# Transfers of 48, 48 and 2 partitions joined into one of 98, and halves of 64 into one of 128, in a Fourier and expert kernel

## The chip, the cores and the metric

The kernel runs on one core of one Trainium2 chip. The metric is the device time of one execution, in microseconds. "Before" is the median of 3 runs. The rows shown come from one profiled execution of the same program.

## What is computed

The input `x` has 8 batches of 3136 rows and 256 columns, in f32. Each batch goes through a real FFT along its rows, a complex 256x256 product with a bias and a soft threshold, and the inverse FFT. Then the 128 rows with the highest gate score go through a small network and are written back in place.

```python
X = np.fft.rfft(x, axis=1)
Yr = Xr @ w_r - Xi @ w_i + b_r
Yi = Xr @ w_i + Xi @ w_r + b_i
Y  = soft threshold of Yr and Yi by 0.01
y  = np.fft.irfft(Y, n=3136, axis=1)
scores = y @ w_gate
top = the 128 rows of the batch with the highest score
y[top] += sigmoid(scores[top]) * (relu(y[top] @ w1) @ w2)
```

## The kernel before

The row index is split as 3136 = 98 x 32, and each transform is done in two stages of matrix products with a transposition between them. The transposition goes through DRAM: the scratch tensor `As[b]` lies between the two forward stages, `Cs[b]` between the two inverse ones. Each tensor of a batch (`x`, `As` written, `As` read, `Cs` written, `Cs` read, output) has 3136 rows of 1 KB, so a batch moves six times 3.1 MB.

- `ld_x` loads a block of `x` (a quarter of a batch) into a tile of 8 KB a partition. 98 classes of rows lie in two groups of 49, at partitions 0 to 48 and 64 to 112. The helper `rows` makes three transfers of it: 48 partitions from 64 on, 48 partitions from 0 on, and the two left over (48 and 112).
- `fold` (GpSimd; VectorE for part of batch 0) makes sums and differences of a block, `s1` multiplies them by the first-stage table `w1f` (TensorE, then a copy to the tile `at` on ScalarE or VectorE), and every second `s1` writes `at` to `As[b]`, through `rows` again (three transfers).
- `ld_a` reads `As[b]` for two steps at a time into the tile `av` (two buffers), in two transfers of 64 partitions. `s2` multiplies it by `g_sb` into the PSUM tile `pm`; ScalarE, VectorE and GpSimd split the result into the high and low parts `Xh` and `Xl`.
- `spectral` is the 256x256 complex product in three passes each (`mm3`, lines 233 to 235), the bias and the threshold. `s2i` is the first inverse stage; it writes `Cs[b]` from `ct` in four transfers of 64 partitions and 128 KB each, for every second step.
- `ld_c` reads `Cs[b]` into the tile `cv` (through `rows`, three transfers), `s1i` is the last stage, and every second `s1i` writes a block of the output from `ot` (through `rows`).

A batch has 13 steps (`G`), and the loop at the end of the function writes out an order by hand: at iteration t come `s1` of a later batch, `ld_a` for step t+2, `ld_x`, `ld_c`, `s2` of step t+1, `s2i` of step t-2, `s1i` of step t-17, and `spectral` of step t, with pieces of routing (`route`: scores, a search for the threshold, the places of the chosen rows) and of the network (`ffn`) between them. Nearly all transfers are issued on SyncE's queue (SP), which works in order. Those issued by `ld` are chained one behind the other; those issued by `put` are placed by the scheduler. Each transfer on SP waits for a semaphore, and eight semaphores go round: a transfer waits until the one issued eight before it has landed.

`place` works out the row numbers of the chosen rows with a chain of small VectorE operations, that ends at line 327.

Of the kernel before, what the change touches and what calls it, by code (L numbers as in the profile page):

```python
# [23 lines left out]
H1 = 49  # L24
LAM = 0.01


def _slots(j):
    out = []
    for a in range(2):  # L30
        if j == NJ - 1:
            out += [(a, False, 49 * a + 98 * k2, 1.0, k2) for k2 in range(17 - a)]
        else:
            for k2 in range(N2):
                k = 2 * j + 2 - a + 98 * k2
                out.append((a, True, k, 1.0 if 2 * k <= S else -1.0, k2))
    return out


def _tables():  # L40
    n1 = np.arange(N1)
    n2 = np.arange(N2)
    w1 = np.zeros((2, H1, N1))
    for a in range(2):
        for j in range(NJ - 1):
            t = 2 * np.pi * ((n1 * (2 * j + 2 - a)) % N1) / N1
            w1[a, 2 * j] = np.cos(t)
            w1[a, 2 * j + 1] = -np.sin(t)
        w1[a, H1 - 1] = 1.0 - 2.0 * a * (n1 % 2)
    g = np.zeros((NJ, 2, 2, N2, 2, N2))  # L50
    gi = np.zeros((NJ, 2, 2, N2, 2, N2))
    for j in range(NJ):
        for a, cplx, k, sg, s in _slots(j):
            t = 2 * np.pi * ((n2 * k) % S) / S
            co, si = np.cos(t), np.sin(t)
            if cplx:
                g[j, a, 0, :, 0, s] = co
                g[j, a, 1, :, 0, s] = si
                g[j, a, 0, :, 1, s] = -sg * si
                g[j, a, 1, :, 1, s] = sg * co  # L60
                gi[j, a, 0, s, 0] = 2 * co / S
                gi[j, a, 1, s, 0] = -2 * sg * si / S
                gi[j, a, 0, s, 1] = 2 * si / S
                gi[j, a, 1, s, 1] = 2 * sg * co / S
            else:
                edge = k in (0, S // 2)
                g[j, a, 0, :, 0, s] = co
                gi[j, a, 0, s, 0] = (1.0 if edge else 2.0) * co / S
                if not edge:
                    g[j, a, 0, :, 1, s] = -si  # L70
                    gi[j, a, 1, s, 0] = -2 * si / S
    main = [v[:NJ - 1].reshape(NJ - 1, 128, 64).transpose(1, 0, 2) for v in (g, gi)]
    g_last = np.zeros((2, N2, 2, 64))
    gi_last = np.zeros((2, 2, N2, 2, N2))
    for a in range(2):
        g_last[a, :, a] = g[NJ - 1, a, 0].reshape(N2, 64)
        gi_last[a, :, :, a] = gi[NJ - 1, a, :, :, 0]
    wf = np.zeros((128, 2, 64))
    wi = np.zeros((128, 64))
    for r in (0, 64):  # L80
        wf[r:r + H1, :, :H1] = w1[:, :, :H1].transpose(2, 0, 1)
    for a in range(2):
        wi[64 * a:64 * a + H1, :H1] = w1[a, :, :H1]
    wq = np.zeros((NJ, 2, 2, N1))
    for gg in range(6):
        for e in range(2):
            for f in range(2):
                for a in range(2):
                    j = 4 * gg + 2 * e + f
                    wq[4 * gg + 2 * f + a, e] = w1[a, 2 * j:2 * j + 2]  # L90
    wq[NJ - 1, 0] = w1[:, H1 - 1]
    return (wf, wi, main[0], main[1], g_last.reshape(64, 2, 64), gi_last.reshape(128, 64), wq.reshape(NJ, 4, N1))
# [19 lines left out]
def fourier_moe(ctx: ExitStack, tc: tile.TileContext, x, w_r, w_i, b_r, b_i, wg, w1, w2,  # L112
# [25 lines left out]
    w1f, w1i = c_tile([128, 2, 64], F32, "w1f"), c_tile([128, 64], F32, "w1i")  # L138
# [69 lines left out]
    def consts_moe(k):  # L208
# [7 lines left out]
        else:  # L216
# [3 lines left out]
            nc.gpsimd.iota(nrow, [[1, 1]], base=0, channel_multiplier=N2, allow_small_or_imprecise_dtypes=True)  # L220
# [61 lines left out]
    def place(b, thr, slots):  # L282
# [25 lines left out]
        for k in range(NCHK):  # L308
# [18 lines left out]
            nc.vector.tensor_tensor(out=idx, in0=c, in1=pi[:, N2 + 1:], op=ALU.add)  # L327
# [86 lines left out]
    def s1(b, i):  # L414
        if i == 0:
            As[b] = dram.tile([2, H1, N2, D], F32, name="As")
# [14 lines left out]
        if i % 2 == 1:  # L431
            rows(put if b else ld, at[b], As[b][:, :, 4 * i - 4:4 * i + 4, :], True)

    def jrows(t, a, j0, n):
        return t[a, 2 * j0:2 * j0 + 2 * n].rearrange("(j q) n d -> (q n) j d", q=2)

    def ld_a(b, g):
        if g == G - 1:
            av[b, g] = pool.tile([64, 1, D], F32, name="av", bufs=2)
            for a in range(2):  # L440
                ld(av[b, g][N2 * a:N2 * a + N2, 0, :], As[b][a, H1 - 1])
        elif g % 2 == 0:
            av[b, g] = av[b, g + 1] = pool.tile([128, 4, D], F32, name="av", bufs=2)
            for k in range(0, 4, 2 if b + g == 0 else 4):
                n = 2 if b + g == 0 else 4
                for a in range(2):
                    ld(av[b, g][64 * a:64 * a + 64, k:k + n, :], jrows(As[b], a, 2 * g + k, n))

    def s2(b, g):
        v = av.pop((b, g))  # L450
        w = width(g)
        px = pm[:, :, :256]
        for p in range(w):
            for h in range(2):
                for e in range(2):
                    for a in range(2):
                        o = px[64 * e:64 * e + 64, a, 64 * (2 * p + h):64 * (2 * p + h) + 64]
                        c = slice(128 * h + 64 * e, 128 * h + 64 * e + 64)
                        if w == 2:
                            r = slice(64 * a, 64 * a + 64)  # L460
                            main_pe[0] = nc.tensor.matmul(o, v[r, 2 * (g % 2) + p, c], g_sb[r, 2 * g + p, :], start=True, stop=True).ins  # L461
                        else:
                            main_pe[0] = nc.tensor.matmul(o, v[:, 0, c], g_last[:, a, :], start=True, stop=True).ins
# [275 lines left out]
```

## Time and profile before

| what | value |
|---|---|
| runs | 995.34, 999.82, 990.12 us (median 995.34) |
| the profiled execution | 992.02 us, of which the span of the trace is 989.7 us |
| mean granted TensorE clock | 0.866 of full speed |
| TensorE busy | 747.6 us (76% of the span) |
| VectorE, ScalarE, GpSimd busy | 535.1, 321.0, 247.0 us |
| moved by the DMA engines | 162.40 MB, 164 GB/s over the span |

The span runs from the first to the last instruction of the core; the 2.3 us outside it are start and end of the execution. Busy TensorE time counts a matmul at either clock. "DMA share" is the mean busy share of the 16 DMA engines; since packets overlap it can read a little over 1.

### The profile page before, as it was taken

What the parts mean: (1) busy time and instruction counts of PE and PEld (TensorE: products, weight loads), DVE (VectorE), ACT (ScalarE), POOL (GpSimd) and SP (SyncE); (2) the same over time, 40 slices, a digit from 0 to 9 for tenths busy, and PEclk for the clock granted to TensorE, in tenths of its full rate; (3) what the DMA queues carried; (4) which work ended last, traced back from release to release, by engine and by line L of the source; (5) the groups of instructions that cost most, each with busy time, mean ns of one, the idle gap of its engine ahead of it and who ended that gap; (6) DMA issues with size and microseconds to landing.
All of it is one profiled execution on the core that took longest, in us unless ns stands there. A gap on an engine that the chain in (4) does not pass through costs nothing.

```text
span 989.7 us, 20397 instructions
## 1 busy us (share of the span) xinstructions
PE 747.6 (76%) x8090; PEld 553.4 (56%) x8090; DVE 535.1 (54%) x1434; ACT 321.0 (32%) x622; POOL 247.0 (25%) x359
## 2 busy tenths in 40 slices
PE   4797888776867787679757986787767867776786
PEld 1375676554745465556546664656546656564456
DVE  5334544445444445345847784654555766766642
ACT  1133333333433433235323442432333332322111
POOL 3054442213133323233322332302300101110001
PEclk9778988888888889789978997979789998988778
DMA  9779788878888787778777877777284773536621
GB/s 172 184 148 216 195 180 162 205 182 219 191 193 189 182 190 210 160 208 194 193 165 189 213 177 172 180 186 160 67 203 102 162 147 79 117 83 137 154 52 46
DMA packets 84188, 162.40 MB, mean 164 GB/s; under 512 B 10593, under 2 KB 64510, under 8 KB 77822
## 3 DMA queue, kind: packets, MB, share of 16 engines
q1 hardware_dynamic: 83054, 158.88, 69.5%
q0 software_dynamic: 896, 2.17, 0.7%
q8 instruction: 64, 1.05, 0.5%
q14 instruction: 30, 0.25, 0.1%
q10 hardware_dynamic: 144, 0.07, 0.0%
HBM read 83.02 MB, written 78.12 MB: 163 GB/s over the span
## 4 chain that ended last, share of the span: by engine, by line
PE 35%; DMA 25%; DVE 15%; SPq 11%; ACT 6%; issue 5%; POOL 1%; POOLq 0%; DVEq 0%; ACTq 0%
DMA av<-As 9%; DMA cv<-Cs 8%; DMA xt<-in_x 7%; SPq L395 6%; PE py L233 5%; PE py L235 5%; SPq L170 5%; PE py L234 4%; PE s L560 4%; PE pm L461 4%; PE s L425 3%; PE s L514 3%; DVE py L489 3%; DVE junk L521 2%; DVE ot L565 1%
## 5 line engine op out<-in xcount | busy, mean ns | idle before, releaser
L461 PE MATMUL pm<-g_sb,av 64*64 64x64 f32 x3072 | 86.7, 244 | 135.0 <-DMA av<-As 103.8
L474 POOL TENSOR_SCALAR Xl<-Xl 128x256 fp32r<-128x256 f32 (+1 forms) x104 | 41.4, 398 | 574.2 <-DVE Xl L473 556.1
L473 DVE TENSOR_TENSOR Xl<-pm,Xh 128x512 fp32r<-128x512 f32 (+1 forms) x104 | 69.6, 669 | 205.4 <-ACT Xh L472 193.4
L461 PEld LDWEIGHTS pm<-g_sb,av 64*64 64x64 f32 x3072 | 73.0, 153 | 186.3 <-issue 78.0
L491 ACT ACTIVATE r<-py,m2l 128x512 f32<-128x512 f32 (+1 forms) x104 | 69.8, 671 | 329.0 <-DVE py L489 215.7
L410 POOL TENSOR_TENSOR x<-xt 113x512 f32<-113x512 f32 x116 | 145.9, 1290 | 25.7 <-DMA xt<-in_x 23.4
L233 PE MATMUL py<-wrh,Xh 128*128 128x256 f32 x400 | 133.2, 333 | 0.0
L233 PEld LDWEIGHTS py<-wrh,Xh 128*128 128x128 f32 x400 | 83.6, 209 | 69.3 <-issue 63.1
L235 PE MATMUL py<-wrl,Xh 128*128 128x256 f32 x400 | 121.3, 303 | 0.0
L234 PE MATMUL py<-wrh,Xl 128*128 128x256 f32 x400 | 120.0, 300 | 0.0
L233 PE MATMUL py<-wih,Xh 128*128 128x256 f32 x400 | 116.6, 291 | 0.0
L234 PE MATMUL py<-wih,Xl 128*128 128x256 f32 x400 | 116.0, 290 | 0.0
L235 PE MATMUL py<-wil,Xh 128*128 128x256 f32 x400 | 115.3, 288 | 0.0
L470 ACT CAST Xh<-pm 128x512 fp32r<-128x512 f32 (+1 forms) x104 | 59.7, 574 | 162.4 <-PE pm L461 147.4
L489 DVE TENSOR_TENSOR py<-py,bias 128x512 f32<-128x512 f32 (+1 forms) x104 | 70.4, 677 | 61.3 <-PE py L235 46.7
L425 PE MATMUL s<-x,w1f 49*64 49x512 f32 x512 | 86.1, 678 | 19.5 <-DVE x L410 13.4
L521 DVE CUSTOM_DVE_ANT_0 junk<-s,wgb 128x256 f32<-128x256 f32 (+1 forms) x200 | 84.4, 422 | 23.9 <-ACT ct L516 19.2
L493 DVE SCALAR_TENSOR_TENSOR Y<-py,r 128x512 f32<-128x512 f32 (+1 forms) x104 | 69.6, 669 | 49.5 <-ACT r L491 49.2
L560 PE MATMUL s<-cv,w1i 49*64 49x512 f32 x480 | 86.2, 731 | 6.7 <-DMA cv<-Cs 5.1
L235 PEld LDWEIGHTS py<-wrl,Xh 128*128 128x128 f32 x400 | 83.8, 210 | 7.5 <-issue 7.2
L234 PEld LDWEIGHTS py<-wrh,Xl 128*128 128x128 f32 x400 | 84.5, 211 | 0.0
L565 DVE TENSOR_TENSOR ot<-even,s 113x512 f32<-113x512 f32 x120 | 78.5, 680 | 7.6 <-ACT even L563 7.5
(117 smaller groups left out, 1186.8 us busy)
## 6 DMA issues: line engine op xcount, KB each, us to landing
xt<-in_x SPq DMA_DIRECT2D x64, 384.0 KB
Cs<-ct SPq DMA_DIRECT2D x192, 128.0 KB
av<-As SPq DMA_DIRECT2D x94, 256.0 KB
As<-at SPq DMA_DIRECT2D x60, 384.0 KB
cv<-Cs SPq DMA_DIRECT2D x60, 384.0 KB
out<-ot SPq DMA_DIRECT2D x60, 384.0 KB
As<-ot SPq DMA_DIRECT2D x4, 384.0 KB
xt<-Cs SPq DMA_DIRECT2D x4, 384.0 KB
```

Of the source, the lines that this page charges most:

```text
L233: nc.tensor.matmul(out, wh, mh, start=start, stop=False)
L234: nc.tensor.matmul(out, wl, mh, start=False, stop=False)
L235: return nc.tensor.matmul(out, wh, ml, start=False, stop=stop).ins
L410: ins = eng.tensor_tensor(out=xs[b, i][:H2, k], in0=t[:, 0], in1=t[:, 1], op=op).ins
L425: main_pe[0] = nc.tensor.matmul(p[64 * e:64 * e + 64, u, :], w1f[r, e, :], x2[r, e, :], start=True, stop=True).ins
L461: main_pe[0] = nc.tensor.matmul(o, v[r, 2 * (g % 2) + p, c], g_sb[r, 2 * g + p, :], start=True, stop=True).ins
L473: step_ins["x"] = nc.vector.tensor_tensor(out=part(xl, 0, 0, 64), in0=pv, in1=part(xh, 0, 0, 64).bitcast(F32), op=ALU.subtract).ins
L489: nc.vector.tensor_tensor(out=py, in0=py, in1=bias.rearrange("p (o d) -> p o d", o=1).broadcast_to([128, w, D]), op=ALU.add)
L491: nc.scalar.activation(out=r1, in_=py, func=AF.Relu, bias=m2l, scale=1.0)
L521: nc.vector.tensor_tensor_reduce(out=junk[:r], in0=p[:r, a, D * f:D * f + D], in1=wgb[:r], scale=1.0, scalar=0.0, op0=ALU.mult, op1=ALU.ad ...
L560: main_pe[0] = nc.tensor.matmul(p[64 * u:64 * u + 64, a, :], w1i[r], c[r, u, o:o + 2, :].rearrange("p c d -> p (c d)"), start=True, stop=T ...
L565: nc.vector.tensor_tensor(out=ot[b][:H2, t, o:o + 2, :].rearrange("p c d -> p (c d)"), in0=even[:H2], in1=p[:H2, 1, :], op=op)
```

## The change

The 98 classes of rows are paired anew, so that a class has its row in one list of 98 for both scratch tensors (`As[b]` and `Cs[b]` become [98, 32, 256]), and they sit on the neighbouring partitions 15 to 112 (`R0` to `H2`) of each tile. With that:

- `x` is laid out on the host by blocks: a block is 98 neighbouring rows of 8 KB in DRAM, and `ld_x` is one transfer of 98 partitions. The output is laid out in the same way, and put back in order on the host.
- A write of `As`, a read of `Cs` and a write of the output are one transfer of 98 partitions each, in place of three. In DRAM a row of such a transfer is 8 KB for all of them; in `As` and `Cs` the rows lie 32 KB apart, as before.
- A read of `As` is one transfer of 128 partitions and 512 KB, in place of two of 64 partitions; a write of `Cs` is one of 128 partitions, in place of four of 64. Their pieces stay at 1 KB.
- The products of `s1` and `s1i` contract over partitions 0 to 63 and 64 to 112; partitions 0 to 14 meet zero weights, and the six tiles of `ring` and `ring_c` are cleared there once at the start (before: three tiles). The number and sizes of all other matmuls stay.
- `cv` becomes three fixed tiles (`ring_c`), one of which takes the fourth block of batch 0, so that all four blocks of batch 0 are loaded at once.
- `Xh` and `Xl` are laid out so that the first copy and the difference are one contiguous piece.
- `place` needs three more small VectorE operations for the new row numbers.

```diff
-    def blocks(v):
-        return v.rearrange("(t n k u c) d -> k u n t (c d)", t=2, n=H1, u=2, c=4)
-
-    def rows(f, t, d, store):
-        for a, b in [(t[64 * u:64 * u + H1 - 1], d[u, :H1 - 1]) for u in (1, 0)] + [(t[H1 - 1:H2:64], d[:, H1 - 1])]:
-            f(b, a) if store else f(a, b)
...
     def ld_x(b, i):
         if i % 2 == 0:
             k = i // 2
-            xt[b, i] = xt[b, i + 1] = ring[(4 * b + k) % XB]
-            if b == 0 and k < XB:
-                (nc.vector, nc.gpsimd)[k % 2].memset(xt[b, i][32:64], 0.0)
-            rows(ld, xt[b, i].rearrange("p t c d -> p t (c d)"), blocks(x[b])[k], False)
+            xt[b, i] = xt[b, i + 1] = ring[(4 * b + k) % XB] if 4 * b + k != XB else ring_c[0].rearrange("p (t c) d -> p t c d", t=2)
+            ld(xt[b, i][R0:H2], x[b, k])
...
+        p_in = (slice(0, 64), slice(64, H2))
...
-                r = slice(64 * u, 64 * u + H1)
+                r = p_in[u]
                 main_pe[0] = nc.tensor.matmul(p[64 * e:64 * e + 64, u, :], w1f[r, e, :], x2[r, e, :], start=True, stop=True).ins
...
-            rows(put if b else ld, at[b], As[b][:, :, 4 * i - 4:4 * i + 4, :], True)
-
-    def jrows(t, a, j0, n):
-        return t[a, 2 * j0:2 * j0 + 2 * n].rearrange("(j q) n d -> (q n) j d", q=2)
+            (put if b else ld)(As[b][:, 4 * i - 4:4 * i + 4, :], at[b][R0:H2])
+
+    def steps(t, g, n):
+        r = H1 * (g // 6) + 8 * (g % 6)
+        return t[r:r + 4 * n].rearrange("(j q) n d -> (q n) j d", q=4)
...
-            for k in range(0, 4, 2 if b + g == 0 else 4):
+            for k in range(0, 2, 1 if b + g == 0 else 2):
                 n = 2 if b + g == 0 else 4
-                for a in range(2):
-                    ld(av[b, g][64 * a:64 * a + 64, k:k + n, :], jrows(As[b], a, 2 * g + k, n))
+                ld(av[b, g][:, 2 * k:2 * k + n, :], steps(As[b], g + k, n))
...
-            for e in range(2):
-                for a in range(2):
-                    nc.sync.dma_start(out=jrows(Cs[b], a, 2 * (g - 1 + e), 2), in_=ct[64 * e:64 * e + 64, :, a, :])
+            put(steps(Cs[b], g - 1, 4), ct.rearrange("p f a d -> p (f a) d"))
...
-            rows(put, cv[b, 2 * k], Cs[b][:, :, 8 * k:8 * k + 8, :], False)
+            cv[b, 2 * k] = cv[b, 2 * k + 1] = ring[k - 2].rearrange("p t c d -> p (t c) d") if b == B - 1 and k > 1 else ring_c[(4 * b + k) % XB]
+            put(cv[b, 2 * k][R0:H2], Cs[b][:, 8 * k:8 * k + 8, :])
...
-            rows(put, ot[b].rearrange("p t c d -> p t (c d)"), blocks(outs[b])[i // 2], True)
+            put(outs[b].rearrange("(k p t c) d -> k p t c d", k=4, t=2, c=4)[i // 2], ot[b][R0:H2])
...
+    ring_c = [pool.tile([128, 8, D], F32, name=f"cv{k}", bufs=1) for k in range(XB)]
+    for k, t in enumerate(ring + ring_c):
+        (nc.vector, nc.gpsimd)[k % 2].memset(t[:32], 0.0)
...
-    for i in range(2 * XB):
+    for i in range(U):
         ld_x(0, i)
...
-            nc.vector.tensor_tensor(out=idx, in0=c, in1=pi[:, N2 + 1:], op=ALU.add)
+            f4 = pool.tile([n, 1], U32, name="f4")
+            nc.vector.tensor_copy(f4, c)
+            nc.vector.tensor_scalar(out=f4, in0=f4, scalar1=2, scalar2=None, op0=ALU.logical_shift_right)
+            nc.vector.tensor_tensor(out=c, in0=c, in1=pi[:, N2 + 1:], op=ALU.add)
+            nc.vector.scalar_tensor_tensor(out=idx, in0=f4, scalar=float(8 * H1 - 4), in1=c, op0=ALU.mult, op1=ALU.add)
```

## Rows read from the trace of the kernel before

**Rows 1.** The page: span, and busy time of each engine.

```profile
span 989.7 us, 20397 instructions
...
PE 747.6 (76%) x8090; PEld 553.4 (56%) x8090; DVE 535.1 (54%) x1434; ACT 321.0 (32%) x622; POOL 247.0 (25%) x359
```

**Rows 2.** The page: chain of work that ended last, by line.

```profile
DMA av<-As 9%; DMA cv<-Cs 8%; DMA xt<-in_x 7%; SPq L395 6%; PE py L233 5%; PE py L235 5%; SPq L170 5%; PE py L234 4%; PE s L560 4%; PE pm L461 4%; PE s L425 3%; PE s L514 3%; DVE py L489 3%; DVE junk L521 2%; DVE ot L565 1%
```

**Rows 3.** Busy time by stretch: length, engines (instructions), clock, DMA share, GB/s.

```profile
0.00:45.00 45.00, 28.65 (x120) 10.51 (x120) 20.35 (x34) 5.39 (x6) 8.29 (x14) 0.89 0.82 174
45.00:130.00 85.00, 70.35 (x818) 57.00 (x818) 37.99 (x81) 30.75 (x60) 39.16 (x50) 0.84 0.84 190
...
331.00:436.00 105.00, 78.59 (x935) 58.99 (x935) 50.58 (x114) 37.25 (x72) 30.92 (x46) 0.85 0.80 190
...
645.00:778.00 133.00, 102.87 (x1064) 76.60 (x1068) 67.68 (x202) 42.30 (x83) 23.68 (x38) 0.87 0.61 142
...
891.00:990.00 99.00, 72.20 (x427) 49.81 (x422) 48.03 (x149) 15.72 (x31) 6.91 (x7) 0.80 0.42 97
```

**Rows 4.** TensorE's waits, whole run: us in total, times, longest.

```profile
PE pm L461 <- DMA av<-As: 103.8, 43, 7.5
```

**Rows 5.** The same for 130 to 436 us, then for 436 to 645 us.

```profile
PE pm L461 <- DMA av<-As: 61.8, 24, 7.5
...
PE pm L461 <- DMA av<-As: 27.6, 10, 6.8
```

**Rows 6.** Timeline of SP, then of TensorE, around one such wait.

```profile
410.13 2.24 SPq L395 DMA_DIRECT2D As<-at  x3
412.42 1.16 SPq L170 DMA_DIRECT2D av<-As  x1
...
418.19 1.02 PE L461 MATMUL pm<-g_sb,av 64*64 64x64 f32 x27 [5.83 <-DMA av<-As]
```

**Rows 7.** Busy time before, in and after that wait, columns as in rows 3.

```profile
405.50:411.50 6.00, 6.00 (x80) 4.50 (x79) 4.00 (x7) 2.31 (x5) 3.78 (x5) 1.00 0.46 109
412.00:418.00 6.00, 0.35 (x3) 0.19 (x2) 1.39 (x2) 0.69 (x1) 0.00 (x0) 0.70 0.90 214
418.00:424.00 6.00, 5.81 (x70) 5.02 (x70) 2.42 (x9) 2.15 (x4) 0.75 (x2) 0.73 0.97 277
```

**Rows 8.** Stretches in which one kind of transfer runs: x, cv, As, Cs, av, w1s, out.

```profile
5.00:18.00 13.00, 7.33 (x28) 2.16 (x30) 6.87 (x16) 1.01 (x1) 2.94 (x2) 1.00 1.05 176
262.40:265.60 3.20, 3.20 (x66) 2.33 (x59) 1.09 (x2) 2.70 (x6) 0.00 (x0) 1.00 1.09 182
249.20:251.20 2.00, 2.00 (x9) 1.54 (x8) 1.02 (x3) 0.93 (x4) 0.48 (x3) 0.50 1.06 213
404.00:406.20 2.20, 2.20 (x19) 2.20 (x19) 1.58 (x6) 0.00 (x0) 2.20 (x3) 0.96 0.95 203
406.80:407.40 0.60, 0.60 (x8) 0.22 (x9) 0.60 (x1) 0.00 (x0) 0.60 (x2) 1.00 0.93 302
192.40:193.40 1.00, 1.00 (x10) 0.49 (x5) 0.71 (x3) 0.59 (x2) 0.74 (x2) 0.92 1.04 406
267.60:269.20 1.60, 0.54 (x35) 0.43 (x30) 1.29 (x5) 0.18 (x1) 0.00 (x0) 1.00 1.01 397
```

**Rows 9.** Issues on SP by tile: ns of one, min/median/max; first and last start.

```profile
L170 SPq DMA_DIRECT2D av<-As x114: 307/616/1886, 40.6 to 869.3; - x114
L395 SPq DMA_DIRECT2D As<-at x84: 302/422/2377, 67.3 to 743.5; - x84
...
L529 SPq DMA_DIRECT2D Cs<-ct x192: 574/607/1508, 74.1 to 902.4; - x192
```

**Rows 10.** Timeline of the start: VectorE's clearing of a tile; TensorE's last pair of `s1`.

```profile
1.32 1.76 DVE L402 MEMSET xt<- 32x2048 f32 x1 [0.46 <-issue]
...
28.13 4.17 PE L425 MATMUL s<-x,w1f 49*64 49x512 f32 x16 [2.01 <-DVE x L410]
```

**Rows 11.** Groups by line: VectorE's last operation of `place`.

```profile
L327 DVE TENSOR_TENSOR idxs<-col,pm 128x1 uint32<-128x1 f32 x8 | 1.2, 154 | 0.2
```

More of the change, by code (lines that the diff above doesn't have):

```diff
@@ L24, with _slots @@
 H1 = 49
+R0 = 15
+H2 = 113
 LAM = 0.01
-def _slots(j):
-    out = []
-    for a in range(2):
[L31 to L37, printed above, removed]
+def _slots(i, a):
+    if i == 24:
+        return [(False, 49 * a + 98 * k2, 1.0, k2) for k2 in range(17 - a)]
+    ks = [2 * i + 2 - a + 98 * k2 for k2 in range(N2)]
+    return [(True, k, 1.0 if 2 * k <= S else -1.0, s) for s, k in enumerate(ks)]
 def _tables():
@@ L44, in _tables @@
     for a in range(2):
[L45 to L48, printed above, removed]
+        for i in range(24):
+            t = 2 * np.pi * ((n1 * (2 * i + 2 - a)) % N1) / N1
+            w1[a, 2 * i] = np.cos(t)
+            w1[a, 2 * i + 1] = -np.sin(t)
         w1[a, H1 - 1] = 1.0 - 2.0 * a * (n1 % 2)
-    g = np.zeros((NJ, 2, 2, N2, 2, N2))
-    gi = np.zeros((NJ, 2, 2, N2, 2, N2))
@@ L52, in _tables @@
[L52 to L71, printed above, removed]
@@ L72, in _tables @@
-    main = [v[:NJ - 1].reshape(NJ - 1, 128, 64).transpose(1, 0, 2) for v in (g, gi)]
+    g = np.zeros((2, 25, 2, N2, 2, N2))
+    gi = np.zeros((2, 25, 2, N2, 2, N2))
+    for a in range(2):
+        for i in range(25):
+            for cplx, k, sg, s in _slots(i, a):
+                t = 2 * np.pi * ((n2 * k) % S) / S
+                co, si = np.cos(t), np.sin(t)
+                if cplx:
+                    g[a, i, 0, :, 0, s] = co
+                    g[a, i, 1, :, 0, s] = si
+                    g[a, i, 0, :, 1, s] = -sg * si
+                    g[a, i, 1, :, 1, s] = sg * co
+                    gi[a, i, 0, s, 0] = 2 * co / S
+                    gi[a, i, 1, s, 0] = -2 * sg * si / S
+                    gi[a, i, 0, s, 1] = 2 * si / S
+                    gi[a, i, 1, s, 1] = 2 * sg * co / S
+                else:
+                    edge = k in (0, S // 2)
+                    g[a, i, 0, :, 0, s] = co
+                    gi[a, i, 0, s, 0] = (1.0 if edge else 2.0) * co / S
+                    if not edge:
+                        g[a, i, 0, :, 1, s] = -si
+                        gi[a, i, 1, s, 0] = -2 * si / S
@@ new lines, in _tables @@
+    tg = np.zeros((2, 64, 24, 64))
+    tgi = np.zeros((2, 64, 24, 64))
+    wq = np.zeros((NJ, 2, 2, N1))
+    for st in range(12):
+        a, c = st // 6, 4 * (st % 6)
+        for j in range(2):
+            for p in range(2):
+                tg[p, :, 2 * st + j] = g[a, c + 2 * j + p].reshape(64, 64)
+                tgi[j, :, 2 * st + p] = gi[a, c + 2 * j + p].reshape(64, 64)
+                r = 2 * (c + 2 * j + p)
+                wq[2 * st + j, p] = w1[a, r:r + 2]
+    wq[NJ - 1, 0] = w1[:, H1 - 1]
@@ L451, in s2 @@
         w = width(g)
-        px = pm[:, :, :256]
-        for p in range(w):
+        for j in range(2):
             for h in range(2):
                 for e in range(2):
[L456 to L463, printed above, removed]
@@ L464, in s2 @@
-        xh, xl = pair([128, 2 * w, 2, 128], "X", 2)
-        pv = px[:, :, :128 * w].rearrange("p a (t c) -> p a t c", c=64)
+                    c = slice(128 * h + 64 * e, 128 * h + 64 * e + 64)
+                    for p in range(w):
+                        o = pm[64 * e:64 * e + 64, p, 128 * h + 64 * j:128 * h + 64 * j + 64]
+                        r = slice(64 * p, 64 * p + 64)
+                        lhs, rhs = (v[r, 2 * (g % 2) + j, c], g_sb[r, 2 * g + j, :]) if w == 2 else (v[:, 0, c], g_last[:, j, :])
+                        main_pe[0] = nc.tensor.matmul(o, lhs, rhs, start=True, stop=True).ins
@@ L467, in part @@
+        xh, xl = pair([128, 2, 2 * w, 128], "X", 2)
+        pv = pm[:, :w, :256].rearrange("p a (t c) -> p a t c", c=64)
         def part(t, k, lo, hi):
-            return t[:, :, k, :].rearrange("p t (a c) -> p a t c", a=2)[:, :, :, lo:hi]
-        nc.scalar.copy(out=part(xh, 0, 0, 64), in_=pv)
+            return t[:, k].rearrange("p (a h) (j c) -> p a (h j) c", a=w, j=2)[:, :, :, lo:hi]
+        whole = [t[:, 0].rearrange("p (a h) c -> p a (h c)", a=w) for t in (xh, xl)]
+        nc.scalar.copy(out=whole[0], in_=pm[:, :w, :256])
@@ L524, in s2i @@
             for a in range(2):
-                nc.sync.dma_start(out=Cs[b][a, H1 - 1], in_=ct[N2 * a:N2 * a + N2, 0, 0, :])
+                put(Cs[b][H1 * a + H1 - 1], ct[N2 * a:N2 * a + N2, 0, 0, :])
         else:
-            for e in range(2):
-                for a in range(2):
-                    nc.sync.dma_start(out=jrows(Cs[b], a, 2 * (g - 1 + e), 2), in_=ct[64 * e:64 * e + 64, :, a, :])
+            put(steps(Cs[b], g - 1, 4), ct.rearrange("p f a d -> p (f a) d"))
     def score(b):
@@ L737 @@
     r = _run(nc, [arrays], core_ids=[0])
-    return np.stack([r.results[0][f"out_{b}"] for b in range(B)])
+    o = np.stack([r.results[0][f"out_{b}"] for b in range(B)])
+    return np.ascontiguousarray(o.reshape(B, 4, 2, H1, 2, 4, D).transpose(0, 4, 3, 1, 2, 5, 6).reshape(B, S, D))
```

66 lines of the change are left out of this document (30 added, 36 removed).

## The prediction, made before the changed kernel was run

> **What bounds the kernel now.** I read the page first. TensorE is the busiest engine, with 747.6 of 989.7 us [rows 1]; no engine is full, so something makes it wait. The chain that ended last names it: transfers and SP's queue (av 9%, cv 8%, xt 7%, the issues of lines 395 and 170 another 11%) take more of it than any line of TensorE [rows 2]. Then busy time by stretch. In one batch of the steady part, 331 to 436 us, TensorE works 78.6 of 105 us while the 16 DMA engines are busy for 0.80 of it, and the granted clock is 0.85 [rows 3]. Of TensorE's waits one stands out: `s2` waits for `av`, 103.8 us in 43 waits, with 7.5 us the longest [rows 4]; 61.8 us of it fall in 24 waits between 130 and 436 us [rows 5]. In 436 to 645 us it is 27.6 us, because the search for the threshold brings other waits.
>
> One such wait shows the mechanism [rows 6]. SP issues the three pieces of an `As` write from 410.13 on, and this takes until 412.37; only then the second half of `av` is issued, at 412.42. TensorE starts on it at 418.19, after 5.83 us of idleness. So the wait is made of SP's issuing, of the `As` bytes ahead in the DMA engines, and of `av` itself. [...]
>
> **The DMA engines.** I looked for stretches in which one kind of transfer runs with the engines full (share near 1) [rows 8]. Loads into 48 partitions are slow: x 176 GB/s, cv 182. The write of `As` from 48 partitions has 213 in its first 2 us. `Cs` has 203, which is about SP's pace, since one of its 131 KB pieces is issued every 607 ns [rows 9] (216 GB/s). `av` has 302. One load into 128 partitions, w1s, has 406, and the write of the output 397. A block is 803 KB (98 rows of 8 KB; 786 KB for `av` and `Cs`), so it now costs x 4.6, cv 4.4, As 3.8, out 2.0, av 2.6, Cs 3.9, together 21.3 us. This agrees with 0.80 of 105 us for four blocks, 21.0 us [rows 3].
>
> After the change x is a load into neighbouring partitions from neighbouring rows, like w1s: I take 354 GB/s, the middle of 302 and 406, so 2.3 us (bounds 2.0, and the 5.2 of the slow rival below). The output takes the same 2.3 us, 0.3 more than now. For cv the destination becomes wide as for w1s while the 8 KB rows stay 32 KB apart in DRAM; no row parts the two, so I take 3.2 us, at 250 GB/s between 354 and 182 (bounds 2.0 and 5.0). For `As` the output shows that rows 32 KB apart can be written at 397, its own row says 213; I take 3.0 us (bounds 2.0 and 4.3). `av` keeps its 1 KB pieces and 2.6 us (bound 1.9 at 406). `Cs` has pieces of the same size and loses SP's pace: 2.6 us (bounds 1.9 and 3.9). Sum 16.0 us a block, bounds 11.8 and 23.3.
>
> [...]
>
> **The wait for av.** Per block SP issues 1 `As` for 3, 1 x, 1 cv and 1 output for 3 each; per two steps 1 `Cs` for 4 and 1 `av` for 2. In the wait above, one `As` issue of 0.42 us [rows 9] for the 2.24 brings `av` forward by 1.8 us. The `As` bytes ahead take 3.0 for 3.8 us, 0.8 less. If `av` stays behind `As` and its first half can no longer go ahead (it is one transfer), its extra 262 KB at 302 GB/s cost 0.9 us. Net 1.7 us less, up to 2.6 where both halves were behind anyway; with a mean wait of 61.8/24 = 2.6 us I take two thirds of the waits as gone: 69 of 103.8 us (bounds: a quarter if `As` takes 4.3 us, and all).
>
> **The clock.** [...]
>
> **Start.** Today's first piece of x goes to partitions from 64 on and waits for nothing; the new first load covers cleared partitions and waits for VectorE's first clearing, until 3.1 us [rows 10]. But four blocks at 176 GB/s take 18 us, at 354 they take 9. The last pair of `s1` starts at 28.13 after waits; four pairs of 4.2 us back to back from about 9 us would start the last at 21.6. I take 6 us (bounds 2 and 9). Three more clearings lie beside the first loads' flight and cost nothing; if VectorE were late for the first `fold`, 1.8 us each.
>
> **End, and edits with small answers.** The last batch reads four blocks of `Cs` at once before its `s1i`: 4 us less if they follow the sum, of which I take 2. `place` has three more operations of 0.154 us [rows 11], only exposed in the last batch: 0.5 us more; in the others VectorE has room (50.6 of 105 us). Matmuls keep number and size; the contraction over 64 for 49 partitions changes no column count, so I cost it at nothing (bounds plus or minus 2 us). The copies to `Xh` and `Xl` have as many elements: nothing, plus or minus 3 us in all, hidden behind `spectral` of the step before.
>
> **What is late next.** When `av` is on time, TensorE meets the chains of ScalarE and VectorE, and the other waits of the search. In 331 to 436 us TensorE is idle for 26.4 us, and about 21 of them are `av` (61.8 x 105/306); 5 us a batch belong to others already. I add 3 us a batch for six batches, 18 us (bounds 5 and 40). The DMA engines would be busy for 64 us of a batch of some 89, so 0.72, no longer the limit.
>
> **Sum.** -69 - 38 - 6 - 2 + 0.5 + 18 = -96.5 us, from the profiled 992.0 to 895.5. The median is 3.3 us above that execution, so 899 us.
>
> **Rivals.** (1) The DRAM side, not the partitions, makes cv and `As` slow. For: x, cv and `As` all have rows 32 KB apart in DRAM, `av` and w1s have not. Against: the output has them, and 397 GB/s. Then only x gains; a block is 2.3 + 5.0 + 4.3 + 2.3 + 2.6 + 2.6 = 19.1 us, SP's issues still shrink, `av` comes 1.8 - 0.5 us earlier and 45% of the waits go: -47 - 20 + 5 = about -62, 933 us. (2) Slower: fewer engines a transfer. The 48-partition transfers keep all 16 engines busy (share 1.05 for x [rows 8]), 3 partitions each. 98 doesn't divide by 16; if 98 partitions are dealt out as 14 shares of 7, two engines stand idle. If moreover each engine keeps today's pace, x, cv and `As` have 154, 159 and 186 GB/s, a block costs 23.3 us, and a batch at today's share of 0.80 takes 93/0.80 = 116 us for 105: 11 us on each of 5.7 batches, 63 us, 1058 us. It decides as soon as a block costs more than 21.3 us, that is if x, cv and `As` stay under some 190 GB/s on average. Against: w1s runs at 406 on the same engines. (3) The waits vanish wholly and the DMA engines have 11.8 us a block: -104 - 51 - 9 - 4 + 15 = -153, 842 us. (4) The scheduler moves the single `av` issue behind `As` and `Cs` each time, or ScalarE's and VectorE's chain takes over the whole gap: 985 to 1000 us.
>
> [...]
>
> **How the numbers follow.** Forecast 0.45 (its own range 870 to 920), rival 1 0.20, rival 3 0.17, rival 4 0.09, rival 2 0.09. The range 838 to 960 reaches nearly to rival 3 and past rival 1, and leaves out rivals 2 and 4. The runs lie within 0.5% of their median, so about 1% is what tells a change from none. Faster by over 1%: 0.45 + 0.20 + 0.17 and a little of rival 4, 0.84; within 1% 0.07; slower 0.09.
>
> **What would show it.** In the trace after: x at over 300 GB/s with the engines full; TensorE's waits for `av` under 50 us in sum; a clock above 0.91 in a steady batch; a batch in 85 to 95 us; the DMA share near 0.7. A share that stays at 0.875 where one kind runs shows 14 engines; cv and `As` near 180 GB/s show rival 1. The prediction is wrong if waits for `av` stay because SP issues it late for another reason, or if VectorE becomes the bound.

## The result, and the profile after

The changed kernel takes 828.4 us (median of 3 runs, 823.5 to 833.5) where the kernel before takes 995.3: a ratio of 0.8325, 95% interval 0.8222 to 0.8429. The forecast was 899 us with a range of 838 to 960, so the sign was right and the gain, 167 us, was 70 us larger than forecast and beyond the end of the range.

The page of the kernel after: span, busy time of each engine, the main DMA queue (packets, MB, its share of 16 engines' span), and the chain that ended last, by line. These answer to [rows 1, 2].

```profile
span 826.6 us, 19849 instructions
PE 682.9 (83%) x8090; PEld 506.1 (61%) x8090; DVE 530.7 (64%) x1461; ACT 316.0 (38%) x622; POOL 252.6 (31%) x361
...
q1 hardware_dynamic: 71134, 158.89, 61.9%
...
DMA xt<-in_x 8%; PE py L239 6%; PE py L241 6%; PE py L240 5%; DMA xe<-in_moe_w 5%; DVE py L489 5%; PE pm L462 4%; DVE junk L521 4%; DVE ot L563 4%; PE s L427 3%; PE s L558 3%; ACT ct L516 2%; ACT Xh L470 2%; DVE Xl L473 2%; POOL x L411 2%
```

The 8090 matmuls are the same number as before, and TensorE is busy with them for 64.7 us less (747.6 to 682.9). Its idle time falls from 989.7 - 747.6 = 242.1 to 826.6 - 682.9 = 143.7 us, 98.4 less. Together that is the whole 163.1 us of span. `av`, `cv` and SP's queue are no longer among the lines of the chain; SP's queue has 1% of it, for 11% before.

Busy time by stretch (columns as in [rows 3]): a steady batch, one with the search for the threshold, and the last batch's end.

```profile
266.10:341.00 74.90, 69.85 (x946) 52.73 (x939) 48.92 (x112) 36.05 (x72) 29.58 (x42) 0.98 0.83 261
...
505.30:620.50 115.20, 94.25 (x1028) 70.15 (x1020) 66.20 (x209) 43.13 (x84) 21.33 (x36) 0.94 0.45 146
735.20:826.60 91.40, 67.84 (x429) 47.55 (x428) 47.67 (x153) 15.92 (x31) 6.86 (x7) 0.87 0.32 105
```

The steady batch took 105 us at a clock of 0.85 [rows 3]; it now takes 74.9 at 0.98, and TensorE is idle for 5.1 of them. It is one of the fastest: by the ends of TensorE's last whole step of `spectral`, batches 1 to 5 (the first is 0) take 74 to 88 us, where they took 96 to 107. The two stretches behind it correspond to 133 and 99 us before [rows 3], so they gain less.

The largest of TensorE's waits over the whole run (us in total, times, longest), to be held against the 103.8 us of [rows 4]; none of the 12 largest is for a transfer:

```profile
PE pm L270 <- DVE n L265: 11.1, 7, 2.7
PE pm L462 <- DVE ok L280: 10.7, 12, 2.3
PE s L427 <- DVE x L411: 9.7, 1, 9.7
```

SP's own waits say why. After:

```profile
SPq L398 <- ACT ct L516: 172.9, 40, 19.1
SPq L173 <- PE pm L462: 147.5, 44, 10.0
```

and the kernel before, the one line for the same wait:

```profile
SPq L170 <- PE pm L461: 16.3, 6, 4.6
```

The second line of the first pair is the load of `av` at the head of SP's queue, waiting for `s2` (L462) to finish with its buffer: in 44 cases, of the 47 loads whose buffer had served such a pair of steps before, the buffer is the last thing that SP waits for. Before, that happened 6 times in a run; in the other cases the buffer was already free and `av` stood behind something else. One such case: the `s2` that freed the buffer, by TensorE's instructions of that line in the kernel before (ns of one, min/median/max; first and last start), and then SP's timeline (start, us, issues):

```profile
L461 PE MATMUL pm<-g_sb,av x64: 216/218/267, 378.6 to 386.6; 64*64 64x64 f32 x64
```

```profile
402.67 2.55 SPq L529 DMA_DIRECT2D Cs<-ct  x4
405.31 0.59 SPq L170 DMA_DIRECT2D av<-As  x1
410.13 2.24 SPq L395 DMA_DIRECT2D As<-at  x3
412.42 1.16 SPq L170 DMA_DIRECT2D av<-As  x1
```

The buffer is free at 386.8, yet the first half is issued at 405.31 behind four `Cs` pieces, and the second at 412.42 behind the `As` write, for which SP stands still from 405.90 to 410.13: 18.5 and 25.6 us late. The same two views of the kernel after:

```profile
L462 PE MATMUL pm<-g_sb,av x128: 216/218/267, 265.3 to 282.8; 64*64 64x64 f32 x128
```

```profile
279.92 0.31 SPq L398 DMA_DIRECT2D As<-at  x1
280.31 1.28 SPq L398 DMA_DIRECT2D Cs<-ct  x2
283.07 0.38 SPq L173 DMA_DIRECT2D av<-As  x1
285.09 0.31 SPq L398 DMA_DIRECT2D cv<-Cs  x1
```

The buffer is free at 283.0 and `av` is issued at 283.07. Taken over the whole pairs whose `s2` starts between 130 and 620 us, without the first of each batch (first issue of a pair less the end of the last `s2` matmul that read its buffer), `av` is issued 16.6 us late on average before and 0.14 us late after.

So two things changed that the diff doesn't name together: the pace, which here means how fast the DMA engines move the same bytes, and the order in which the scheduler queued the transfers on SP.

### The profile page after: what moved, and what is told of

Same layout as the page of the kernel before. It is cut to its first block, busy times and chain, and to the rows that moved or that the text cites. A ratio compares the mean times of both kernels' runs of the same rounds, so it can differ in the third digit from the quotient of the medians.

```text
span 826.6 us, 19849 instructions
## 1 busy us (share of the span) xinstructions
PE 682.9 (83%) x8090; PEld 506.1 (61%) x8090; DVE 530.7 (64%) x1461; ACT 316.0 (38%) x622; POOL 252.6 (31%) x361
## 4 chain that ended last, share of the span: by engine, by line
PE 36%; DVE 25%; DMA 15%; ACT 11%; issue 8%; POOL 3%; SPq 1%; POOLq 0%; DVEq 0%; ACTq 0%
DMA xt<-in_x 8%; PE py L239 6%; PE py L241 6%; PE py L240 5%; DMA xe<-in_moe_w 5%; DVE py L489 5%; PE pm L462 4%; DVE junk L521 4%; DVE ot L563 4%; PE s L427 3%; PE s L558 3%; ACT ct L516 2%; ACT Xh L470 2%; DVE Xl L473 2%; POOL x L411 2%
## 5 line engine op out<-in xcount | busy, mean ns | idle before, releaser
L239 PE MATMUL py<-wrh,Xh 128*128 128x256 f32 x400 | 126.5, 316 | 0.0
L240 PE MATMUL py<-wrh,Xl 128*128 128x256 f32 x400 | 114.8, 287 | 0.0
L239 PEld LDWEIGHTS py<-wrh,Xh 128*128 128x128 f32 x400 | 78.1, 195 | 59.1 <-issue 55.0
L462 PEld LDWEIGHTS pm<-g_sb,av 64*64 64x64 f32 x3072 | 61.2, 141 | 78.2 <-DVE ok L280 24.3
L427 PE MATMUL s<-x,w1f 64*64 64x512 f32 (+1 forms) x512 | 81.2, 655 | 27.2 <-DVE x L411 9.7
L493 DVE SCALAR_TENSOR_TENSOR Y<-py,r 128x512 f32<-128x512 f32 (+1 forms) x104 | 69.5, 668 | 50.8 <-ACT r L491 50.6
L462 PE MATMUL pm<-g_sb,av 64*64 64x64 f32 x3072 | 69.9, 230 | 30.6 <-DVE ok L280 10.0
L241 PEld LDWEIGHTS py<-wrl,Xh 128*128 128x128 f32 x400 | 78.4, 196 | 4.7 <-issue 4.3
L240 PEld LDWEIGHTS py<-wih,Xl 128*128 128x128 f32 x400 | 76.9, 192 | 6.1 <-POOL Xl L475 6.1
L558 PE MATMUL s<-cv,w1i 64*64 64x512 f32 (+1 forms) x480 | 71.4, 634 | 10.1 <-DVE at L430 5.3
L240 PEld LDWEIGHTS py<-wrh,Xl 128*128 128x128 f32 x400 | 78.6, 197 | 1.3 <-issue 1.3
```

What stands on the lines that cost most here:

```text
L239: nc.tensor.matmul(out, wh, mh, start=start, stop=False)
L240: nc.tensor.matmul(out, wl, mh, start=False, stop=False)
L241: return nc.tensor.matmul(out, wh, ml, start=False, stop=stop).ins
L462: main_pe[0] = nc.tensor.matmul(o, lhs, rhs, start=True, stop=True).ins
L558: main_pe[0] = nc.tensor.matmul(p[64 * u:64 * u + 64, a, :], w1i[r, u, :], c[r, u, o:o + 2, :].rearrange("p c d -> p (c d)"), start=True, ...
```

## The experiments

Eighteen kernels were run, each with three timed rounds against the kernel before on the same chip (996 to 1002 us there). The table holds what the argument needs. "Engine time" is q1's share times the span, the time that the transfers of SP keep 16 engines busy. "Moved" counts, over the block transfers (x, `As`, `av`, `Cs`, `cv`, output) in the order in which SP executes them, pairs within 80 places that stand the other way round than in the kernel after. "Late" is the mean lateness of `av` as worked out above. "Wait" is TensorE's wait for `av` on the line of `s2`'s matmuls for whole steps, whole run.

| run | SP issues | engine time us | moved | late us | wait us | time us | ratio to before |
|---|---|---|---|---|---|---|---|
| before | 740 | 688 | 307 | 16.6 | 103.8 | 995 | 1 |
| after | 291 | 512 | 0 | 0.1 | 0 | 828 | 0.833 |
| e1, by columns | 738 | 518 | 13 | 1.1 | 0 | 834 | 0.832 [0.824, 0.839] |
| e5, x rows apart | 291 | 509 | 0 | 0.2 | 0 | 830 | 0.827 [0.820, 0.834] |
| e2, by halves | 740 | 684 | 314 | 17.0 | 105.0 | 994 | 0.990 [0.981, 0.999] |
| e4, 96 + 2 | 419 | 545 | 268 | 9.9 | 54.8 | 889 | 0.887 [0.881, 0.894] |
| e15, 84 + 14 | 419 | 534 | 268 | 10.4 | 65.7 | 900 | 0.904 [0.898, 0.910] |
| e12, `av`, `Cs` by halves | 484 | 553 | 149 | 3.6 | 10.6 | 841 | 0.845 [0.840, 0.850] |
| e13, the 98s by halves | 547 | 637 | 305 | 14.0 | 87.5 | 965 | 0.969 [0.961, 0.978] |
| e14, every second partition | 740 | 535 | 311 | 15.2 | 76.7 | 933 | 0.937 [0.931, 0.943] |
| e16, before, `av` ahead of `As` | 740 | 682 | 300 | 16.1 | 75.8 | 982 | 0.985 [0.978, 0.993] |
| e17, e2, the same | 740 | 682 | 307 | 16.0 | 71.1 | 964 | 0.969 [0.960, 0.979] |
| e20, e14, the same | 740 | 534 | 304 | 14.8 | 50.6 | 914 | 0.920 [0.911, 0.929] |
| e19, after, the same | 291 | 510 | 0 | 0.1 | 0 | 829 | 0.831 [0.822, 0.839] |
| e21, before, `av` first | 740 | 697 | 277 | 5.2 | 18.2 | 984 | 0.989 [0.974, 1.004] |
| e22, e2, `av` first | 740 | 693 | 279 | 5.3 | 27.8 | 982 | 0.986 [0.973, 1.000] |
| e23, e14, `av` first | 740 | 546 | 284 | 4.4 | 12.0 | 928 | 0.929 [0.913, 0.944] |
| e24, after, `av` late | 291 | 517 | 188 | 13.9 | 87.0 | 929 | 0.931 [0.918, 0.944] |
| e25, e14 in after's order | 740 | 533 | 0 | 2.5 | 0 | 865 | 0.866 [0.859, 0.873] |
| e26, e2 in after's order | 740 | 669 | 0 | 5.0 | 21.0 | 905 | 0.906 [0.900, 0.912] |

The rows of e23's profile come from an execution of 939 us, 11 above its median.

**First round: how many transfers, which pieces, which layout.** The kernel after was cut apart again in different ways. In e1 each transfer is three of the same 98 partitions (two for `av`, four for `Cs`):

```
+    cols = lambda f, t, d, store: [f(*((d[:, p:q], t[R0:H2, p:q]) if store else (t[R0:H2, p:q], d[:, p:q]))) for p, q in ((0, 4), (4, 7), (7, 8))]
-            ld(xt[b, i][R0:H2], x[b, k])
+            cols(ld, xt[b, i].rearrange("p t c d -> p (t c) d"), x[b, k].rearrange("p t c d -> p (t c) d"), False)
```

> The changed kernel with every transfer of 98 partitions issued as three (columns of 4, 3 and 1 KB a partition), av as two and Cs as four: the partitions stay wide and the bytes the same, but SP has to issue as many transfers as before the change. Theory A (the number of transfers on SP's queue, with at most eight in flight, held av back): the waits for av come back, some 60 to 100 us of them, and the time goes to 920 to 990 us. Theory B (the pace of transfers into 48 or 64 partitions held it back): the pace stays, so 825 to 860 us and next to no waits for av.

In e2 the pieces are by partitions, as before, while x and the output stay in blocks:

```
+    halves = lambda f, t, d, store: [f(*((d[s], t[R0:H2][s]) if store else (t[R0:H2][s], d[s]))) for s in (slice(49, 97), slice(0, 48), slice(48, N1, 49))]
```

> The changed kernel with the joining alone undone: pieces of 48, 48 and 2 partitions for 98, halves of 64 for 128, as many transfers as before; x and the output stay in blocks of neighbouring rows. Theory A: like e1_cols within 2%. Theory B: 940 to 1000 us, well above e1_cols. If the layout of x in blocks were what counted, it stays near 830 to 860 us.

`av` and `Cs` go by halves of 64 there. In e4 the same line has `slice(0, 96), slice(96, 98)`, and `av` and `Cs` stay whole.

> The changed kernel with each transfer of 98 partitions issued as one of 96 and one of 2, so that all 16 engines can share the first (6 partitions each for 7 on 14): pace of the engines up by up to a seventh, 128 more transfers on SP. Theory A: 828 to 850 us (more issues, nothing gained). Theory B, with the engines still the limit at a busy share of 0.83: 800 to 822 us.

In e5 the transfers are untouched and x is laid out in DRAM so that a block's rows lie 32 KB apart (`x[b, :, k]` for `x[b, k]`).

> The changed kernel with the rows of a block of x 32 KB apart in DRAM, as those of As and Cs are, for 8 KB apart; every engine's order of instructions is the same. If rows 32 KB apart made x slow before (176 GB/s), x falls from some 265 to under 200 GB/s and the time rises by 1 to 4%. If the partitions made it slow, x keeps its pace and the time stays within 1%.

e1 has as many issues as the kernel before and 834 us: the number of transfers is not the cause. (SP's issues last 388 us in sum there, for 500 in the kernel before and 150 in the kernel after.) e5 takes away the neighbourhood of x's rows in DRAM and loses nothing; `As` and `Cs` keep their rows 32 KB apart, and the mean 8 KB packet falls all the same, from 609 ns before (`As` and `cv` alone) to 416 after. So rival 1 falls. e2 gives nearly the whole gain back (994), so x in blocks, and all else that e2 keeps of the change, is worth about 1%. What counts is how the pieces lie over the partitions. e4 with two pieces is in between (889, outside both of its theories), although its engine time is near that of the kernel after.

**Second round: pace apart from pieces.** e14 has e2's pieces in number and size, but each takes every second partition (`slice(1, 96, 2), slice(0, 96, 2), slice(96, 98)`, `av` and `Cs` `[a::2]`); e15 has e4's two pieces as 84 and 14; e12 splits `av` and `Cs` alone, e13 the transfers of 98 alone.

> e2_halves with every second partition in each piece: 98 is issued as 48 odd rows, 48 even rows and 2, 128 as two sets of 64 with a step of 2. Number and size of the transfers, engines for each, and nearly the order on every engine are those of e2_halves; only the spread of a piece over the partitions is that of the changed kernel. Pace theory (a piece inside one half of the partitions is slow): the mean pace returns to some 250 GB/s in the steady part and the time to 825 to 900 us. Order theory (the scheduler's order that comes with the pieces costs the time): it stays at 960 to 1000 us.

> e4_96_2 with the pieces of 84 and 14 partitions for 96 and 2; every engine has the same order of instructions as in e4_96_2. If the order of e4_96_2 is what costs it 60 us, 875 to 900 us. If the transfer of 2 partitions is what costs them, 828 to 845 us.

> The changed kernel with the joining undone for av (two halves of 64 partitions) and Cs (four) alone. Pace theory: 840 to 880 us, a small part of the gain lost, since their packets are a third of the engines' work. If the wait for av is what the whole gain hangs on, and av's own halves make it: 930 us or more.

> The changed kernel with the joining undone for the transfers of 98 partitions alone (48, 48 and 2 for x, As, cv and the output); av and Cs stay one transfer of 128. Pace theory: 930 to 985 us, most of the gain lost. If av's and Cs's joining made the gain: 830 to 870 us.

The main queue on the pages (packets, MB, share) of e2, then of e14:

```profile
q1 hardware_dynamic: 76782, 158.91, 68.8%
```

```profile
q1 hardware_dynamic: 76782, 158.91, 57.6%
```

The same packets and bytes take 684 us of 16 engines in e2 (0.688 x 994.5) and 535 in e14 (0.576 x 929.6), and the time falls from 994 to 933 with the order of the queue as it was (314 and 311 moved; against the kernel before, only 4 and 9 pairs). That is the pace by itself: 61 us, which lies between the pace theory and the order theory put on record for e14. What the two runs differ in is where a large piece lies: in e2 within partitions 0 to 63 or within 64 to 127, in e14 over both. But TensorE still waits 76.7 us for `av` in e14, and e4 and e15 wait 55 and 66 us with two pieces at a good pace (545 and 534 us of engine time); e4's order is e15's, and their times differ by 10 us, so the piece of 2 partitions is not what e4 suffers from. So something other than pace is left, and "moved" and "late" go with it.

**Third round: `av` ahead of the `As` write.** In the timeline of the kernel before the second half stood behind `As`, so the call that loads `av` was moved ahead of the one that writes `As` in the step loop, in the kernel before (e16), e2 (e17), e14 (e20) and the kernel after (e19):

```
+        if t + AP >= G:
+            at_step(t + AP, ld_a, G)
         run(t, s1, LEAD)
...
-        if t + AP >= G:
-            at_step(t + AP, ld_a, G)
```

> The kernel before, with one edit: in the step loop the load of av is issued ahead of the run that issues the As write and the other transfers, so that no load of av stands behind an As write in SP's queue. Theory C (two causes: av stood behind a waiting As write in SP's queue, worth most of TensorE's waits for av, and the two-half pieces move slowly, worth some 60 us): the waits for av fall from 104 us to under 40, and the time falls to 900 to 950 us. Theory P (pace alone; the place in the queue is not what makes av late): waits within 15 us of 104 and the time within 1% of before, 985 to 1005. Theory Q (the pace was only slow because of what av's lateness made collide): 830 to 860.

> The kernel after with each transfer taken apart again by partitions (48, 48 and 2; halves of 64), as in the run e2, and the load of av issued ahead of the As write. Theory C: as for the kernel before with that edit, 900 to 950 us (e2: 994), since layout of x in blocks was worth only 1%. Theory P: 994 within 1%. Theory Q: 830 to 860.

> The kernel after with each transfer taken apart into every second partition (48, 48 and 2; 64 and 64), as in the run e14, and the load of av issued ahead of the As write. This has as many transfers as the kernel before and full pace. Theory C: both causes are gone, so the waits for av are under 15 us and the time is 828 to 860 us (e14: 933, 77 us of waits). Theory P: 933 within 1%.

> The kernel after, whole transfers, with the load of av issued ahead of the As write. Theory C: here no av stands behind an As write anyway, so 828 us within 1%. Theory P: the same. If it falls by over 1%, some of the after kernel's time still hangs on that order.

The gains in e16, e17 and e20 are 14, 30 and 19 us: theory C missed by far, and the times lie 3 to 20 us below theory P's. The edit moved little. In SP's order in the kernel before, the first piece of `av` comes right behind an `As` write in 8 of 56 loads, behind `Cs` in 30 and behind the output in 12; the edit takes away 7 of the 8. So 300 to 307 pairs are still the other way round and `av` is still 15 to 16 us late. The runs say that the place right behind `As` alone is not the cause, and leave the order as a whole open.

**Fourth round: `av` alone put early, or late.** e21 (before), e22 (e2) and e23 (e14) give the load of `av` priority; e24 queues each `av` of the kernel after behind the last write on SP (`put` keeps each in `put_ins`).

```
+            with tc.high_priority():
                 at_step(t + AP, ld_a, G)
```

```
-                ld(av[b, g][:, 2 * k:2 * k + n, :], steps(As[b], g + k, n))
+                with tc.issue_after(put_ins[-1]) if b > 0 else ExitStack(): ld(av[b, g][:, 2 * k:2 * k + n, :], steps(As[b], g + k, n))
```

> The kernel before, the loads of av given priority, so that in SP's queue they stand where the kernel after has them: in the kernel before 1.33 MB more of As, Cs and output stand ahead of each av than in the kernel after, and its first piece is issued 16.6 us after its buffer came free (after: 0.1). Theory C (late av and slow pace, two causes): av is issued within 3 us of its buffer coming free, TensorE's waits for av fall from 104 to under 25 us, and the pace of the pieces (609 ns for 8 KB) stays slow, so that a batch needs some 84 us of the DMA engines: 900 to 945 us. Theory P (the pace alone makes av late): waits and time within 2% of before, 975 to 1005. Theory O (the order alone): 825 to 850.

> The run e2 (pieces of 48, 48 and 2 partitions and halves of 64, x and output in blocks) with the same priority for av. Theory C: 895 to 940 us (e2 994), waits under 25 us. Theory P: 975 to 1000. Theory O: 825 to 850.

> The run e14 (every second partition; full pace, 740 transfers) with the same priority for av: neither slow pace nor late av. Theory C: 828 to 855 us (e14 933), waits for av under 12 us. Theory P: 925 to 940. Theory O: as theory C.

> The kernel after with each load of av queued behind the last write on SP, so that 1.43 MB more of As, Cs and output stand ahead of it, as in the kernel before, at the full pace and with whole transfers. Theory C: av is issued 8 to 15 us late, TensorE waits for av 45 to 80 us and the time is 880 to 935 us. Theory P: within 2% of 828. Theory O: 960 to 1000.

TensorE's two largest waits for transfers in e21:

```profile
PE s L560 <- DMA cv<-Cs: 53.7, 12, 9.9
PE pm L461 <- DMA av<-As: 18.2, 18, 2.6
```

and SP's wait for `av`'s buffer in e21, to be held against 147.5 us in 44 waits in the kernel after:

```profile
SPq L170 <- PE pm L461: 116.5, 17, 16.6
```

In e21 this wait for `av` is down from 103.8 to 18.2 us (on all lines, from 108.4 to 33.7), but the one for `cv` grew from 5.1 to 53.7, and the time is the same within the interval. Now SP sits up to 16.6 us at one `av` whose buffer isn't free (20.9 in e23, 10.0 at most in the kernel after), and `cv` stands behind it. e22 and e23 show the same with 54.5 and 41.5 us for `cv`. All three missed theory C's time; their times are those of theory P, though `av`'s waits fell nearly as in C. Here one place in the queue could not be mended without the others. Against this, e24 shows that the order is enough to lose the gain: whole transfers at full pace (517 us of engine time) with `av` 13.9 us late take 929 us, 101 more than the kernel after and within theory C's range; the waits of 87.0 us are above its 45 to 80.

```profile
PE pm L462 <- DMA av<-As: 87.0, 20, 6.3
```

**Fifth round: the whole order.** The 240 block transfers of the kernel after, in SP's order, were written down as a string of kinds, and e14 and e2 had theirs queued in that order, with no other edit:

```
+    line = [i for k in ORDER for i in units[k].pop(0)]
+    for a, b in zip(line, line[1:]):
+        tc.add_manual_dep(b, a.name, mybir.DependencyInfo(mybir.DependencyClass.NoSync, mybir.DependencyReason.DATA), reason="order")
```

> The run e14 (every second partition, 740 transfers, full pace, 933 us) with all 240 block transfers on SP (x, As, av, Cs, cv and output) queued in exactly the order in which the kernel after has them, none but these moved. Theory C (order and pace): no transfer is late any more, neither av nor cv, so waits for av and cv under 10 us each and 828 to 850 us. If the number of transfers or SP's time for them matters after all: 880 to 935.

> The run e2 (48, 48 and 2 partitions and halves of 64, slow pace, 994 us, within 1% of the kernel before) with all 240 block transfers queued in the kernel after's order. It is the kernel before's way of moving data with only the order changed. Theory C: the pace stays at some 580 ns for 8 KB, a batch needs some 84 us of the DMA engines and cannot go much under 90: 890 to 945 us. Order alone (the pace doesn't matter): 828 to 850. Pace alone: 975 to 1000.

TensorE's longest waits in e26, where `av` heads the list, and then those of e25, where no transfer is among the first twelve:

```profile
PE pm L476 <- DMA av<-As: 21.0, 14, 4.0
PE pm L272 <- DVE n L267: 15.6, 10, 2.6
```

```profile
PE pm L544 <- DVE Csc L535: 14.0, 5, 3.4
PE pm L272 <- DVE n L267: 13.9, 9, 2.2
```

Pace and order now make a table, in us, all with 740 issues:

| | order as before | order as after |
|---|---|---|
| pieces in one half each (e2, e26) | 994 | 905 |
| pieces over both halves (e14, e25) | 933 | 865 |

The order is worth 89 us at the slow pace and 68 at the full one; the pace 61 and 40; both 129. e26 came out in theory C's range (890 to 945). e25 did not: its waits for `av` and `cv` are gone as expected, but 865 is 15 us above the range, between its two theories, and 31 above e1, which has as many issues and nearly the same order. e25's idle time is 157.0 us (866.3 - 709.3) for 143.7, and its matmuls take 26.4 us longer at a clock of 0.911 for 0.944. In e1 the operations of the compute engines also run nearly in the order of the kernel after; in e25 they don't (0.98 to 1.00 of each engine's sequence matches in e1; 0.88 of TensorE's and 0.53 of GpSimd's in e25). SP's issues also last longer in sum, 458 us in e25 for 388 in e1. Whether the 31 us lie in either was not tried and stays open.

No version tried beats the kernel after: e19 and e5 are level with it.

## Why the prediction was wrong

**DMA engines: the sum was right.** It said 16.0 us a block for 21.3. In the steady batch it is 0.83 x 74.9 / 4 = 15.5, over the run 512 / 32 = 16.0 with the constants in it. By packets it holds as well: 8 KB packets (x, `As`, `cv`, output) take 416 ns on average, so a block of the four is 4 x 98 x 0.416 / 16 = 10.2 us of 16 engines for 10.8 forecast, and 1 KB packets (`av`, `Cs`) take 53 ns, 2 x 768 x 0.053 / 16 = 5.1 for 5.2. x itself was taken too fast (354 GB/s). At the start it moves at 307 in the first 2 us and then, with some constants beside it, at 237 to 266 (busy time by stretch, kernel after, columns as in [rows 3]):

```profile
5.00:7.00 2.00, 0.00 (x0) 0.00 (x0) 1.62 (x2) 0.00 (x0) 1.39 (x3) 1.00 0.89 307
7.00:9.00 2.00, 0.00 (x0) 0.00 (x0) 0.35 (x7) 0.00 (x0) 0.00 (x0) 1.00 0.91 237
9.00:11.00 2.00, 1.25 (x6) 0.63 (x10) 2.00 (x4) 0.00 (x0) 0.00 (x0) 1.00 0.92 250
11.00:13.00 2.00, 2.00 (x14) 0.60 (x8) 1.03 (x2) 0.63 (x1) 0.51 (x1) 1.00 0.85 266
```

That is still well above 176 [rows 8]. The shares of 0.85 to 0.92 would fit rival 2's 14 of 16 engines (0.875). The packets' times fit it too: from 5 to 13 us of the kernel after, SP's queue has most often 14 packets in flight at once (5.4 of the 8 us), where the kernel before has most often 16 from 5 to 18 us (6.3 of the 13 us). But no view shows the engines one by one. What rival 2 needed besides, the old pace for each engine, did not hold: the pace rose (609 to 416 ns for 8 KB). e4, with 96 of 98 partitions in one transfer, doesn't settle the 14 engines, since its queue has another order.

Two readings of rows behind these terms need putting right. The prediction put the slow pace down to 48 partitions; e14 moves pieces of 48 with 535 us of engine time in all, for e2's 684, so what counts between these two is that e2's lie in one half. Why the output, in the same pieces, had 397 GB/s stays open. And the 302 GB/s for `av` is the middle of one half's flow: its 256 packets run from 406.70 to 407.83 us, 262 KB at 232 GB/s, near half of w1s's 406. So `av` is no counterexample.

**The wait for `av`: the step that failed.** The prediction kept `av` behind `As` in SP's queue, worked out by how much the shorter issues and the faster bytes bring it forward (1.7 of a mean 2.6 us), and let a third of the waits stay: -69. All went: -103.8, and 4.6 more of the last step's `av`. The fault is in taking the place in the queue as given. [rows 6] shows `av` behind `As`, and the timeline above that SP stood still for `As`; the prediction counted the issue behind it, and not that the buffer had been free for 25 us by then. With whole transfers the scheduler queued them in another order, with `av` ahead of what waits, and it is then 0.14 us late. The pace alone, at the old order, takes TensorE's waits for `av` only from 105.0 to 76.7 us (e2, e14). e24 is the shortest proof, and the nearest run to what the prediction assumed: whole transfers at full pace with `av` kept behind writes leave 87.0 us of waits and take 929 us. That the forecast's 69 us came as near to 103.8 as they did is in part luck: the mechanism behind them removes less, and the order removed the rest. Rival 4 named this mechanism, that the scheduler's order moves `av`, and looked at the bad side only (985 to 1000).

**The clock: the same step carried on.** The sum has -38 for it, and the sums of rivals 1 and 3 have -20 and -51. No run shows these terms, as none changes the clock by itself; what the runs show in their place is this. The granted clock has two levels, 1.00 and 0.50 of full speed. Around the wait of [rows 6, 7] it is 1.00 from 404.5 to 414.0 us, thus into the wait, and 0.50 from 414.5 to 421.0, in the rest of it and in the first work behind it. A matmul of line 234 takes 279 ns at 1.00 and 415 at 0.50, and the next one starts 118 and 213 ns after it (medians, kernel before). The clock is at 0.50 for 264.7 us before and 92.6 after, and TensorE is busy in 200.6 and 79.4 of them. An estimate from this: (200.6 - 79.4) x (1 - 118 / 213) = 54 us, most of the 64.7 by which TensorE's busy time fell for the same matmuls. In three runs the mean clock and the waits for `av` go together: 0.866 with 103.8 us before, 0.882 with 87.0 in e24, 0.944 with none after; e21 has 0.868 with 18.2, and 53.7 for `cv`. All the waits went, and more busy time than forecast.

**What is late next: too dark.** 18 us of other waits were added. TensorE's idle time apart from `av` is 133.7 us before (242.1 - 108.4) and 143.7 after, so 10 us came; in the steady batch it is 5.1 us for the forecast's 5 + 3.

**Start and end.** -6 and -2 were forecast. The first `spectral` step has its bias added by 46.2 us for 53.8, 7.6 less. The end, from the last whole step of `spectral` on, takes 91.4 us for 99.0, 7.6 less. These lie within the idle and busy time above and are not added to it.

**The sum as it came out:** -98.4 of idle time and -64.7 of busy time make -163.1. The forecast's -96.5 differs by 66.6, of which `av` is 39.4 (108.4 less 69) and TensorE's busy time 26.7 (64.7 less the clock's 38); the rest cancels to about 0.5.

**The signs that were asked for.** Waits for `av` under 50 us, the clock above 0.91: yes. x above 300 GB/s: only in the first 2 us. A batch in 85 to 95 us: 75. DMA share near 0.7: 0.83, since the batch is shorter at the same bytes. The rivals: 1 falls by e5; 2 by the pace; 3 came nearest (842, waits wholly gone), but with 11.8 us a block for a measured 15.5 to 16.0, so its nearness is in part luck.

**What stays open.** Why the scheduler orders the queue differently for pieces by partitions than for whole transfers or pieces by columns: e12 (149 moved) and e13 (305) say that the transfers of 98 partitions decide most of it, and e1 that their number doesn't; the runs show no more. Also open is the 31 us between e25 and e1.

## What to carry to other kernels

Where one in-order queue issues all transfers, look for each load at what its issue waits for. If that is the buffer, its place is right; if the buffer is long free, it is its place in the queue that is late, and faster bytes need not mend that (15.2 us late in e14, for 17.0 in e2). A change to the shape of transfers can also change the order that a scheduler gives them, so compare the queue's order before and after building, ahead of any sum over bytes, and give the order a price of both signs. In e21 to e23 a single load given priority only moved the wait to the next one.

## What was not expected of the hardware

Pieces of every second partition move nearly as fast as whole transfers: SP's transfers keep 16 engines busy for 535 us in e14 and for 512 in the kernel after. As many pieces, the large ones in one half of the partitions each, take 684 us in e2. 447 more issues on SP, e1 against the kernel after, cost nothing clear of the noise: 0.832 of the kernel before, for 0.833.
